# Attention in two-chunk operations over adjacent PSUM banks, with PSUM as one tile and operands in 4 KB pairs

## The chip, the cores and the metric

One core of one Trainium2 chip runs the whole program. The metric is the device time of an execution in microseconds; the time given for a kernel is the median of its runs. TensorE appears in the profile as PE (matmuls) and PEld (weight loads), VectorE as DVE, ScalarE as ACT, GpSimd as POOL, and SyncE, which issues the DMAs, as SP.

## What is computed

Two batches of 3008 tokens go through an attention without softmax and then through two feed-forward layers (256 to 2048 to 256), all in float32.

```python
def _attn_ref(u, v, z):
    scores = (1.0 / S) * np.matmul(z, z.transpose(0, 2, 1))   # S = 3008, z has 64 columns
    attn = np.maximum(scores, 0.0) ** 2
    return u * np.matmul(attn, v)                             # v and u have 256 columns

def _moe_ref(x, w_in, w_out):
    h = x @ w_in
    return np.where(h > 0.0, h, np.exp(np.minimum(h, 0.0)) - 1.0) @ w_out

def _moe2_ref(x, w_in, w_out, a, b):
    h = x @ w_in
    P = a[0] + a[1] * h + a[2] * h**2 + a[3] * h**3
    Q = 1.0 + np.abs(b[0]) * np.abs(h) + np.abs(b[1]) * h**2
    return (P / (Q + 1e-06)) @ w_out
```

## The kernel before

Each float32 operand of a matmul is held as a rounded part (hi, r) and a remainder (lo, l), and each product is three matmuls (hi times hi, lo times hi, hi times lo). So most of the work of the other engines is making such pairs.

*Attention.* The queries are cut into 12 tiles (`spans`), six per batch, of 512 columns; the sixth of each batch has 448. The keys are cut into 24 chunks of 128 rows, the last half full; a step n is one chunk of one tile, and there are NA = 288 steps. The 64 channels of z lie twice on the partitions, so scores for two chunks run on the two row halves of PE at once. At every even step `pair` (L249) issues the six score matmuls for chunks n and n+1 into two banks of PSUM. `scores` (L263) then does for one chunk: ScalarE's relu (L270, PSUM to SBUF), ScalarE's square of it (L273, the hi part), and VectorE's product of score and relu (L277), written over the score in PSUM, for the first eight chunks into SBUF. One step later `scores_lo` (L281) subtracts the hi part from that product (L285, VectorE), which gives the lo part and leaves the bank free. `values` (L288) follows LAG = 4 steps behind the scores: twelve matmuls per chunk (L303), six in the half-full one, into four banks, one for each half of the model columns and each row half. At the end of a tile VectorE multiplies two of these banks by u (L309), ScalarE copies the two others (L310), POOL multiplies and adds (L312, L313) and the tile is stored to DRAM (L314).

*Weights.* Each weight arrives as 64-bit words and is turned into a pair by ScalarE (L177, L194, L195), VectorE (the words step L181 and L183, the powers step L188 and L190, one chunk step apart) and POOL (L199 to L206). 32 half-megabyte pieces are spread over the attention steps by a list of due steps, `todo`: 12 of them during the first batch, between the second batch's values, stored to DRAM and read back by `stages_reload` from step NA on, and 20 directly during the second batch, straight into the pool `wp` of 64 operands of 2 KB per partition. That pool also holds the values, as hi and lo.

*Feed-forward.* 13 token tiles (384, ten of 512, two of 256 columns) go through both layers in one pipeline of steps (`ffn_step`, L563); a step has one group of 128 hidden rows of the first layer and, three steps behind the tile, one of the second. Line numbers: `hidden` L358 (L363, L364, L366), `project` L369 (through L231 to L233), the first layer's exponential L390 and L391, ELU L396 and split L402 (ScalarE) and L403 (POOL), the second's polynomial L436 to L493. The last tile's steps are put in order by a small planner (`finish`).

*Order.* The program is written under a manual schedule: each engine executes its instructions in the order in which the code issues them. In step n that is scores(n), scores_lo(n-1), what `todo` holds for n, values(n-4), then the feed-forward step. PSUM's eight banks come from a pool of eight one-bank tiles; SBUF operands come from small pools by tag (x 6, rl 4, x2 4, hi 3, lo 3, r 2, q 3, e 3, t 3 of 2 KB).

```python
    for n in range(NA + NSTEP):
        if n < NA:
            scores(n)
        if 0 < n <= NA:
            scores_lo(n - 1)
        for fn in todo.pop(n, ()):
            fn()
        if LAG <= n < NA + LAG:
            values(n - LAG)
```

## Time and profile before

| | |
|---|---|
| median of 3 runs | 1635.21 us (1633.59 to 1637.61) |
| the profiled execution | 1636.99 us |
| its span in the profile | 1635.2 us |
| mean granted clock of PE | 0.988 |
| PE busy | 1582.3 us (97%), 9240 matmuls |
| DVE busy | 1407.3 us (86%), 2148 instructions |
| ACT busy | 1342.6 us (82%), 2321 |
| POOL busy | 751.5 us (46%), 595 |
| DMA | 63.46 MB in 40000 packets, 12.1% of 16 engines |

Busy time is the union of an engine's instructions. Matmuls are pipelined and their ends are modelled, so a PE that is shown busy may still be waiting in part; two matmuls on the two row halves run at once and are shown as two overlapping instructions. A wait is put down to the instruction that ended last before it. Clock 1.00 is the full granted clock.

### The profile page before, as it was taken

To read this page: it belongs to the slowest core of one execution; us is meant where nothing else is said; L and a number is where in the kernel's file an instruction comes from. 1 tells how busy PE (TensorE), PEld (TensorE's weight loads), DVE (VectorE), ACT (ScalarE), POOL (GpSimd) and SP (SyncE) were. 2 spreads that over 40 slices of the span, in tenths; PEclk is the share of its full clock that TensorE was granted. 3 is DMA by queue.
4 is the path that set the end of the run, shared out by engine and by line. 5 is a ranking of instruction groups with operands and counts; after the bars stand their busy time and mean duration, and the time that the engine had idled before them with its cause. 6 is when DMAs were issued, how large, how long until landed. Compare 5 with 4: busy or idle time off the path is not lost.

```text
span 1635.2 us, 25774 instructions
## 1 busy us (share of the span) xinstructions
PE 1582.3 (97%) x9240; PEld 1299.7 (79%) x9240; DVE 1407.3 (86%) x2148; ACT 1342.6 (82%) x2321; POOL 751.5 (46%) x595
## 2 busy tenths in 40 slices
PE   8999999999999999999999999999999999998897
PEld 6877778777878878878878787878788787887796
DVE  7788888998987368888898989898898989899998
ACT  7788777787886688989888888888898888887796
POOL 3334341433443445444444544444444445447645
PEclk9999999999999999999999999999999999999998
DMA  4223233112221410000000000000000000000000
GB/s 129 71 93 127 87 112 118 58 54 72 78 78 48 140 52 1 23 1 27 1 1 27 1 26 1 27 0 27 0 27 1 1 20 1 20 0 14 1 14 13
DMA packets 40128, 65.09 MB, mean 40 GB/s; under 512 B 5440, under 2 KB 18240, under 8 KB 40000
## 3 DMA queue, kind: packets, MB, share of 16 engines
q1 hardware_dynamic: 40000, 63.46, 12.1%
q8 instruction: 72, 1.18, 0.3%
q14 instruction: 56, 0.46, 0.1%
HBM read 44.83 MB, written 18.61 MB: 39 GB/s over the span
## 4 chain that ended last, share of the span: by engine, by line
PE 69%; DVE 11%; ACT 4%; issue 3%; POOL 1%; DMA 0%; POOLq 0%; DVEq 0%; ACTq 0%
PE acc L232 10%; PE acc L233 10%; PE h L363 10%; PE h L364 10%; PE acc L231 10%; PE h L366 10%; PE acc L303 9%; PE s L259 3%; DVE lo L285 1%; DVE s L277 1%; DVE x L486 1%; ACT e L270 1%; DVE q L465 1%; DVE raw L181 1%; DVE t L488 1%
## 5 line engine op out<-in xcount | busy, mean ns | idle before, releaser
L493 POOL TENSOR_TENSOR x<-t,r 128x512 fp32r<-128x512 f32 (+1 forms) x190 | 250.2, 1317 | 479.3 <-DVE t L488 459.3
L303 PE MATMUL acc<-hi,v 64*128 64x512 f32 (+1 forms) x1364 | 255.0, 393 | 3.9 <-DVE x L285 2.3
L403 POOL TENSOR_TENSOR lo<-e,hi 128x512 fp32r<-128x512 f32 (+1 forms) x192 | 246.0, 1282 | 24.9 <-ACT hi L402 24.9
L277 DVE SCALAR_TENSOR_TENSOR s<-s,e 128x512 f32<-128x512 f32 (+1 forms) x280 | 191.4, 684 | 64.6 <-ACT e L270 60.9
L270 ACT ACTIVATE e<-s 128x512 f32<-128x512 f32 (+1 forms) x288 | 167.0, 580 | 74.1 <-PE s L259 72.2
L436 ACT ACTIVATE t<-h,coef 128x512 f32<-128x512 f32 (+1 forms) x192 | 148.0, 771 | 82.5 <-PE h L366 82.4
L303 PEld LDWEIGHTS acc<-hi,v 64*128 64x128 f32 x1364 | 188.8, 187 | 31.8 <-DVE xo L309 3.2
L303 PE MATMUL acc<-lo,v 64*128 64x512 f32 (+1 forms) x682 | 204.8, 391 | 1.2 <-DVE lo L285 1.2
L463 DVE SCALAR_TENSOR_TENSOR q<-q,coef,h 128x512 f32<-128x512 f32 (+1 forms) x166 | 122.0, 735 | 83.3 <-ACT q L456 83.3
L303 PE MATMUL acc<-r,v 64*128 64x512 f32 (+1 forms) x892 | 166.8, 390 | 5.0 <-DVE lo L285 3.3
L232 PE MATMUL acc<-x,w 128*128 128x512 f32 (+2 forms) x416 | 158.2, 380 | 7.7 <-POOL x L493 7.5
L232 PE MATMUL acc<-lo,w 128*128 128x512 f32 (+2 forms) x416 | 157.7, 379 | 5.2 <-POOL lo L403 4.9
L363 PE MATMUL h<-x,w 128*128 128x512 f32 (+2 forms) x416 | 155.2, 376 | 5.0 <-DVE t L488 5.0
L231 PE MATMUL acc<-x,w 128*128 128x512 f32 (+2 forms) x416 | 157.1, 378 | 3.1 <-DVE t L488 3.1
L233 PE MATMUL acc<-x,w 128*128 128x512 f32 (+2 forms) x416 | 157.2, 378 | 0.0
L363 PE MATMUL h<-rl,w 128*128 128x512 f32 (+2 forms) x416 | 154.9, 376 | 2.3 <-DVE e L396 1.6
L233 PE MATMUL acc<-hi,w 128*128 128x512 f32 (+2 forms) x416 | 156.2, 375 | 0.0
L231 PE MATMUL acc<-hi,w 128*128 128x512 f32 (+2 forms) x416 | 156.0, 375 | 0.0
L364 PE MATMUL h<-x,w 128*128 128x512 f32 (+2 forms) x416 | 155.2, 376 | 0.0
L364 PE MATMUL h<-rl,w 128*128 128x512 f32 (+2 forms) x416 | 154.5, 375 | 0.0
L396 DVE SCALAR_TENSOR_TENSOR e<-e,h 128x512 f32<-128x512 f32 (+1 forms) x192 | 128.5, 669 | 27.1 <-ACT e L391 27.1
L303 PEld LDWEIGHTS acc<-r,v 64*128 64x128 f32 x892 | 122.6, 184 | 23.7 <-ACT q L310 3.5
(107 smaller groups left out, 4416.2 us busy)
## 6 DMA issues: line engine op xcount, KB each, us to landing
raw<-w_in_dram SPq DMA_DIRECT2D x16, 512.0 KB, 4.0
raw<-w_out_dram SPq DMA_DIRECT2D x16, 512.0 KB, 4.6
wd<-q SPq DMA_DIRECT2D x24, 256.0 KB, 2.3
raw<-wd SPq DMA_DIRECT2D x12, 512.0 KB, 3.4
raw<-v_dram SPq DMA_DIRECT2D x22, 256.0 KB, 3.7
raw<-uT_dram SPq DMA_DIRECT2D x10, 512.0 KB, 4.2
xd<-xo SPq DMA_DIRECT2D x20, 256.0 KB, 2.0
outT_dram<-xo SPq DMA_DIRECT2D x20, 256.0 KB, 2.1
```

The costliest lines, as they stand in the source:

```text
L231: nc.tensor.matmul(out, lhsT=lh, rhs=rh, start=start, stop=False)
L232: nc.tensor.matmul(out, lhsT=lh, rhs=rl, start=False, stop=False)
L233: nc.tensor.matmul(out, lhsT=ll, rhs=rh, start=False, stop=stop)
L270: nc.scalar.activation(p[:, :w], s[:, :w], AF.Relu, scale=SCALE)
L277: nc.vector.scalar_tensor_tensor(out=q[:, :w], in0=s[:, :w], scalar=SCALE, in1=p[:, :w], op0=ALU.mult, op1=ALU.mult)
L303: nc.tensor.matmul(acc[ti][d][h][:, :w], lhsT=lhs[rows, j % 2, d * P:(d + 1) * P], rhs=rhs[rows, :w], start=j == 0 and k == 0, stop=j >= N ...
L363: nc.tensor.matmul(h[:, cols], lhsT=wh[:, d, c], rhs=x[d][0], start=d == 0, stop=False)
L364: nc.tensor.matmul(h[:, cols], lhsT=wl[:, d, c], rhs=x[d][0], start=False, stop=False)
L366: nc.tensor.matmul(h[:, cols], lhsT=wh[:, d, c], rhs=x[d][1], start=False, stop=d == ND - 1)
L403: nc.gpsimd.tensor_tensor(out=lo, in0=e, in1=f(hi), op=ALU.subtract)
L436: act(new("p", "t", 3), h, AF.Identity, bias=a2, scale=a3)
L493: tt(out=st["lo"], in0=st["p"], in1=st["r"], op=ALU.mult)
```

## The change

The two chunks of a pair get one operation each for relu, square, product and subtraction, 1024 columns over two adjacent banks (512 per bank). PSUM becomes one tile of eight banks. During attention scores use banks 0 to 3 in turn (n % 4) and the accumulators 4 to 7; in the feed-forward part the kernel hands banks out from a list and takes them back after the last reader (`bank`, `give`), and where the list is empty before `first_hidden`, the ELU is issued ahead of it. All operand buffers become pairs of 4 KB: `wp` has 32 of them, and the relu's output is taken from there. The tile's accumulators are read in two halves: two banks before the matmuls of its last chunk, two after. The last tile's four final operations run on VectorE in place of POOL. 18 weight pieces are kept directly and 14 stored and read back, from step NA-4 on; the first feed-forward input is split at step NA-3 in place of NA-1.

```diff
-    wp = ctx.enter_context(tc.tile_pool(name="wp", bufs=64))
+    wp = ctx.enter_context(tc.tile_pool(name="wp", bufs=32))
...
-    ps = ctx.enter_context(tc.tile_pool(name="ps", bufs=8, space=bass.MemoryType.PSUM))
+    ps = ctx.enter_context(tc.tile_pool(name="ps", bufs=1, space=bass.MemoryType.PSUM))
...
+    def sb2(tag, bufs, dt=F32R):
+        return sp.tile([P, 2, W], dt, tag=tag, bufs=bufs, name=tag)
+
+    def wide(dt=F32R):
+        return wp.tile([P, 2, W], dt, tag="w", name="w")
+
+
+    psum = ps.tile([P, 8, W], F32, tag="psum", name="psum")
+    free_banks = []
+    banks_of = {}
+
+    def bank(key):
+        i = free_banks.pop(0)
+        banks_of.setdefault(key, []).append(i)
+        return psum[:, i]
+
+    def give(key):
+        free_banks.extend(banks_of.pop(key))
...
-            r = sb("x", 6, F32R)
-            l = sb("rl", 4, F32R) if s < 4 else sb("t", 3, F32R)
+            if s < 4:
+                rl = sb2("rl", 2) if s < 2 else sb2("x2", 2)
+                r, l = rl[:, 0], rl[:, 1]
+            else:
+                r, l = (sb("t", 3, F32R) if s == 4 else sb("r", 2, F32R) for _ in range(2))
...
+            if keep:
+                st["t"] = wide()
+            st["hi"] = st["t"][:, 0] if keep else sb("q", 3, F32R)
...
-    def pair(n):
+    def scores(n):
 
         ti, j = divmod(n, NCH)
         bb, i0, w = spans[ti]
         r, l = Z[bb, i0 // W]
         sr, sl = Z[bb, j // 4]
-        out = sc[n], sc[n + 1] = bank("s"), bank("s")
+        i = n % 4
+        s = psum[:, i:i + 2, :w]
         for k, (lhs, rhs) in enumerate(((sr, r), (sl, r), (sr, l))):
             for h in range(2):
                 rows, c = slice(h * DQ, (h + 1) * DQ), (j + h) % 4 * P
-                nc.tensor.matmul(out[h][:, :w], lhsT=lhs[rows, c:c + P], rhs=rhs[rows, :w], start=k == 0, stop=k == 2)
-
-    sc = {}
-
-    def scores(n):
-        ti, j = divmod(n, NCH)
-        bb, i0, w = spans[ti]
-        if j % 2 == 0:
-            pair(n)
-        s = sc.pop(n)
-        p = sb("e", 3)
-        nc.scalar.activation(p[:, :w], s[:, :w], AF.Relu, scale=SCALE)
-        spare = n % (LAG + 1) > 2
-        hi = sb("r", 2, F32R) if spare else sb("hi", 3, F32R)
-        nc.scalar.activation(hi[:, :w], p[:, :w], AF.Square)
-
-
-        q = sb("t", 3) if n < 8 else s
-        nc.vector.scalar_tensor_tensor(
-            out=q[:, :w], in0=s[:, :w], scalar=SCALE, in1=p[:, :w], op0=ALU.mult, op1=ALU.mult)
-        hl[n] = hi, q
+                nc.tensor.matmul(s[:, h], lhsT=lhs[rows, c:c + P], rhs=rhs[rows, :w], start=k == 0, stop=k == 2)
+        hi = sb2("hl", 3)
+        e = wide(F32)[:, :, :w]
+        nc.scalar.activation(e, s, AF.Relu, scale=SCALE)
+        nc.scalar.activation(hi[:, :, :w], e, AF.Square)
+
+        nc.vector.scalar_tensor_tensor(out=s, in0=s, scalar=SCALE, in1=e, op0=ALU.mult, op1=ALU.mult)
+        hl[n] = hi
 
     def scores_lo(n):
         w = spans[n // NCH][2]
-        hi, q = hl[n]
-        lo = sb("x2", 4, F32R) if n % (LAG + 1) > 2 else sb("lo", 3, F32R)
-        nc.vector.tensor_tensor(out=lo[:, :w], in0=q[:, :w], in1=f(hi[:, :w]), op=ALU.subtract)
-        hl[n] = hi, lo
+        hi, lo = hl.pop(n), sb2("x", 3)
+        i = n % 4
+        nc.vector.tensor_tensor(
+            out=lo[:, :, :w], in0=psum[:, i:i + 2, :w], in1=f(hi[:, :, :w]), op=ALU.subtract)
+        for h in range(2):
+            hl[n + h] = hi[:, h], lo[:, h]
+        if n >= NA - 4:
+            free_banks.extend((i, i + 1))
 
     def values(n):
         ti, j = divmod(n, NCH)
         bb, i0, w = spans[ti]
         if j == 0:
 
-            acc[ti] = [[bank("acc") for _ in range(2)] for _ in range(ND)]
+            acc[ti] = {way: psum[:, 4 + k] for k, way in enumerate(((1, 0), (0, 1), (0, 0), (1, 1)))}
         hi, lo = hl.pop(n)
         vh, vl = V[bb, j // 2]
-
-
-        ways = ((0, 1), (1, 0)) if j < NCH - 1 else ((0, 1),)
-        for way in ways:
+        if j == NCH - 1:
+            xd[ti] = dp.tile([P, ND, W], F32, tag=f"xd{ti}", name=f"xd{ti}")
+            out_of(ti, 1, w)
+
+
+        for way in ((1, 0), (0, 1))[j == NCH - 1:]:
             for k, (lhs, rhs) in enumerate(((vh, hi), (vl, hi), (vh, lo))):
                 for h, d in enumerate(way):
                     rows = slice(h * P // 2, (h + 1) * P // 2)
-                    nc.tensor.matmul(acc[ti][d][h][:, :w], lhsT=lhs[rows, j % 2, d * P:(d + 1) * P], rhs=rhs[rows, :w],
-                                     start=j == 0 and k == 0, stop=j >= NCH - 2 and k == 2 and (h != d or j == NCH - 1))
+                    nc.tensor.matmul(
+                        acc[ti][d, h][:, :w], lhsT=lhs[rows, j % 2, d * P:(d + 1) * P], rhs=rhs[rows, :w],
+                        start=j == 0 and k == 0, stop=k == 2 and j == NCH - 1 - (h != d))
         if j == NCH - 1:
-            xd[ti] = dp.tile([P, ND, W], F32, tag=f"xd{ti}", name=f"xd{ti}")
-            x, y = [sb("xo", 2)[:, :w] for _ in range(ND)], [sb("q", 3)[:, :w] for _ in range(ND)]
+            x, y = out_of(ti, 0, w)
+
+            eng = nc.gpsimd if ti < NTL - 1 else nc.vector
             for d in range(ND):
-                nc.vector.tensor_tensor(out=x[d], in0=acc[ti][d][0][:, :w], in1=us[ti][:, d, :w], op=ALU.mult)
-                nc.scalar.copy(y[1 - d], acc[ti][1 - d][1][:, :w])
-            for d in range(ND):
-                nc.gpsimd.tensor_tensor(out=y[d], in0=y[d], in1=us[ti][:, d, :w], op=ALU.mult)
-                nc.gpsimd.tensor_tensor(out=x[d], in0=x[d], in1=y[d], op=ALU.add)
+                eng.tensor_tensor(out=y[d], in0=y[d], in1=us[ti][:, d, :w], op=ALU.mult)
+                eng.tensor_tensor(out=x[d], in0=x[d], in1=y[d], op=ALU.add)
                 nc.sync.dma_start(out=xd[ti][:, d, :w], in_=x[d])
-            del acc[ti], us[ti]
+            del acc[ti], us[ti], sums[ti]
...
+    sums = {}
+
+    def out_of(ti, d, w):
+
+        x, y = sums.setdefault(ti, ({}, {}))
+        x[d], y[1 - d] = sb("xo", 2)[:, :w], (sb("t", 3) if d else sb("e", 3))[:, :w]
+        nc.vector.tensor_tensor(out=x[d], in0=acc[ti][d, 0][:, :w], in1=us[ti][:, d, :w], op=ALU.mult)
+        nc.scalar.copy(y[1 - d], acc[ti][1 - d, 1][:, :w])
+        if ti == NTL - 1:
+            free_banks.extend((4, 5) if d else (6, 7))
+        return x, y
...
-        hi, lo = ([sb("rl", 4, F32R)[:, :w] for _ in range(ND)] for _ in range(2))
+        hi, lo = ([t[:, d, :w] for d in range(ND)] for t in (sb2("rl", 2), sb2("rl", 2)))
...
-        hi, lo = sb("hi", 3, F32R)[:, :flat(i)], sb("lo", 3, F32R)[:, :flat(i)]
+        t = sb2("hl", 3)
+        hi, lo = t[:, 0, :flat(i)], t[:, 1, :flat(i)]
...
-            new("hi", "x", 6, F32R)
+            two(("hi", "lo"), wide() if last else sb2("x", 3))
...
+        reads = {"linear", "size", "denominator", "numerator"} if plain else {"quotient"}
+
+        def then_free(name, fn):
+            def run():
+                fn()
+                if name in reads:
+                    reads.remove(name)
+                    if not reads:
+                        give(("h", 1, i))
+            return run
...
+        elu = [i1] if i1 else []
         if i:
+            if not free_banks:
+                first_elu(elu.pop())
...
-    direct, stored = order[:NF + 4], order[NF + 4:]
-    halves = [x for pair in zip(((1, g) for g in range(NCH // 2)), stored) for x in pair]
+    direct, stored = order[:NF + 2], order[NF + 2:]
+    halves = [x for g, key in enumerate(stored) for x in ([(1, g), key] if g < NCH // 2 else [key])]
...
-        at(NA + 3 * k // 2, AHEAD, stages_reload(*key))
+        at(NA - 4 + 3 * k // 2, AHEAD, stages_reload(*key))
...
-        if n < NA:
+        if n < NA and n % 2 == 0:
             scores(n)
-        if 0 < n <= NA:
+        if n < NA and n % 2:
...
-        if n == NA - 1:
+        if n == NA - 3:
```

## Rows read from the trace of the kernel before

**Rows 1.** Stretches: length, busy us per engine (count), granted clock, DMA share, GB/s
```profile
5.13:538.30 533.17, 512.70 (x4267) 416.50 (x4268) 456.32 (x754) 413.13 (x727) 207.57 (x167) 0.99 0.27 86
538.30:620.00 81.70, 76.57 (x372) 69.11 (x373) 46.76 (x83) 64.08 (x126) 40.84 (x37) 0.96 0.26 90
620.00:1300.00 680.00, 679.70 (x2935) 547.89 (x2934) 604.76 (x896) 593.40 (x1008) 323.35 (x253) 1.00 0.04 11
...
1590.00:1636.00 46.00, 34.28 (x236) 32.35 (x236) 37.92 (x55) 28.50 (x49) 24.45 (x19) 0.87 0.04 12
```

**Rows 2.** Chain that ended last, 300 to 340 us: start, us, what
```profile
304.62 0.69 PE s L259 x6
305.31 2.79 PE acc L303 x24
```

**Rows 3.** Who waited for whom, 20 to 560 us: total, times, longest
```profile
PEld s L259 <- DVE lo L285: 14.8, 21, 2.1
...
PEld s L259 <- DVE x L285: 8.1, 14, 1.0
...
PEld acc L303 <- DVE xo L309: 6.2, 10, 2.0
```

**Rows 4.** Stretches: the start; three of the eleven tile turns, and their sum
```profile
5.13:30.15 25.02, 22.55 (x163) 15.95 (x163) 22.44 (x35) 20.10 (x36) 10.22 (x8) 1.00 0.49 141
...
96.26:100.80 4.54, 4.22 (x34) 2.89 (x32) 4.38 (x9) 4.34 (x8) 2.86 (x3) 1.00 0.07 23
...
182.74:190.61 7.87, 5.55 (x32) 3.89 (x30) 6.43 (x12) 4.56 (x9) 4.42 (x4) 0.78 0.09 34
...
494.09:500.58 6.49, 5.44 (x33) 4.01 (x30) 5.25 (x10) 5.05 (x10) 6.33 (x6) 0.76 0.01 3
sum 59.61, PE 49.33 PEld 34.33 DVE 55.48 ACT 48.39 POOL 42.84; mean PE 4.48 PEld 3.12 DVE 5.04 ACT 4.40 POOL 3.89
```

**Rows 5.** Timeline of one pair: start, us, engine, line, [idle before <- releaser]
```profile
177.16 0.39 PE L303 MATMUL acc<-hi,v 64*128 64x512 f32 x1
...
177.36 0.60 ACT L270 ACTIVATE e<-s 128x512 f32<-128x512 f32 x1 [1.00 <-PE s L259]
...
177.99 0.70 DVE L277 SCALAR_TENSOR_TENSOR s<-s,e 128x512 f32<-128x512 f32 x1 [0.93 <-ACT e L270]
...
178.60 0.68 DVE L285 TENSOR_TENSOR lo<-s,hi 128x512 fp32r<-128x512 f32 x1
...
179.20 0.69 DVE L277 SCALAR_TENSOR_TENSOR s<-s,e 128x512 f32<-128x512 f32 x1
```

**Rows 6.** Groups by line and shape: busy us, mean ns, idle before, releasers
```profile
L277 DVE SCALAR_TENSOR_TENSOR s<-s,e 128x512 f32<-128x512 f32 x232 | 161.3, 695 | 51.8 <-ACT e L270 48.1
...
L270 ACT ACTIVATE e<-s 128x512 f32<-128x512 f32 x240 | 141.3, 589 | 60.4 <-PE s L259 59.3
...
L285 DVE TENSOR_TENSOR lo<-s,hi 128x512 fp32r<-128x512 f32 x138 | 93.9, 681 | 0.0
...
L277 DVE SCALAR_TENSOR_TENSOR s<-s,e 128x448 f32<-128x448 f32 x48 | 30.1, 628 | 12.9 <-ACT e L270 12.8
...
L270 ACT ACTIVATE e<-s 128x448 f32<-128x448 f32 x48 | 25.7, 536 | 13.7 <-PE s L259 12.9 <-DVE rl L119 0.8
...
L181 DVE SCALAR_TENSOR_TENSOR raw<-q,raw 128x512 f32<-128x512 f32 x32 | 24.3, 759 | 0.0
...
L183 DVE TENSOR_SCALAR q<-raw 128x512 uint32<-128x512 uint32 x32 | 18.5, 578 | 2.3
```

**Rows 7.** Timeline at the end of attention, POOL and PE
```profile
543.06 1.19 POOL L313 TENSOR_TENSOR xo<-xo,q 128x448 f32<-128x448 f32 x1
...
544.22 1.94 POOL L403 TENSOR_TENSOR lo<-e,hi 128x384 fp32r<-128x384 f32 x2
...
545.26 0.69 PE L232 MATMUL acc<-lo,w 128*128 128x384 f32 x1 [2.50 <-POOL lo L403]
```

**Rows 8.** Timeline in the late feed-forward part, one matmul
```profile
1477.50 0.39 PE L363 MATMUL h<-rl,w 128*128 128x256 f32 x1 [1.62 <-DVE e L396]
```

More of the change, by code (lines that the diff above doesn't have):

```diff
@@ L147, in split @@
             raw = st["raw"]
-            hi, lo = (wp.tile([P, 2, DM], F32R, tag="w", name="v") for _ in range(2))
+            t = wide()
+            hi, lo = (t[:, i].rearrange("p (c d) -> p c d", c=2) for i in range(2))
             nc.scalar.copy(hi, raw)
@@ L221, in copy @@
         def copy():
-            hl = [wp.tile([P, W], F32R, tag="w", name="w") for _ in range(2)]
+            t = wide()
+            hl = [t[:, i] for i in range(2)]
             nc.scalar.copy(hl[0], st["raw"][:, 0])
@@ L357, in hidden @@
     def hidden(which, x, i):
-        h = bank("h")
+        h = bank(("h", which, i))
         for k, cols in blocks(i):
@@ L372, in project @@
         if n == 0:
-            acc[which, ti] = [bank("acc") for _ in range(ND)]
+            acc[which, ti] = [bank(("acc", which, ti)) for _ in range(ND)]
         steps = [(d, k, cols) for k, cols in blocks(i) for d in range(ND)]
@@ L410, in split_x2 @@
             p = acc[0, ti][d][:, :w]
-            hi, lo = (sb("x2", 4, F32R)[:, :w] for _ in range(2))
+            t = sb2("x2", 2)
+            hi, lo = t[:, 0, :w], t[:, 1, :w]
             nc.scalar.copy(hi, p)
@@ L414, in split_x2 @@
             x2[ti].append((hi, lo))
+        give(("acc", 0, ti))
     def second_hidden(i):
@@ L433, in new, with two @@
             return st[key]
+        def two(keys, t):
+            for i, key in enumerate(keys):
+                st[key] = t[:, i, :n]
         def linear():
@@ L439, in square @@
             if last:
-                new("s", "s2", 0), new("r", "r", 0)
+                two("sr", wide(F32))
             elif late(i):
@@ L450, in size @@
             if last:
-                st["q"] = bank("q")[:, :n]
+                st["q"] = bank(("h", 1, i))[:, :n]
             else:
@@ L505, in second @@
             ]
-        return [
+            return listed()
+        steps = [
             ("square", "A", 0.85, ["hidden"], square),
@@ L516, in second @@
         ]
+        return listed()
     def late(i):
```

21 lines of the change are left out of this document (10 added, 11 removed).

## The prediction

> **What bounds the kernel now.** I read the stretches first, then the chain of waits, then who waited for whom, then single instructions. The stretches [rows 1] cut the span at the first scores matmul, at the end of the last attention matmul and at the stalls of the end. In the middle of the feed-forward part PE is busy 679.70 of 680 us: nothing that this change does on other engines can shorten that. In the attention stage PE shows 512.70 of 533.17 us, but the ends of matmuls are modelled, so I price the stage from the chain: where it runs freely, two chunks cost 0.69 us of scores and 2.79 us of values [rows 2], 3.48 us. A tile is 12 such pairs less three matmul pairs (the half chunk at its end, 0.70), 41.1 us; the two tiles of 448 columns come to about 36.2 (448/512 of it and a little). Ten and two make 483.4 us; the stretch also holds about 3 us of early feed-forward matmuls. So attention loses 533.2 - 483.4 - 3.2 = **46.6 us** to waits of PE, and that is all the change can win there.
>
> Where are they? PE waits before scores for VectorE's L285, 14.8 and 8.1 us in 35 times, and before values for L309, 6.2 us [rows 3]. Eleven tile turns, each from the fifth chunk's scores to the seventh's, take 59.61 us together, the wide ones between 4.54 and 7.87 each [rows 4]; nine cost 3.48 and two narrow ones about 3.06 without waits, 37.4 in all, so the turns lose **22.2 us**. The other 24.4 us are the start (25.02 us [rows 4] for two scores and five pairs, 18.8: some 6) and single waits in the middle of tiles (some **18**).
>
> Why single waits? Follow one pair [rows 5]. PE goes on from scores to values at 177.16, the relu starts at 177.36, the product at 177.99, the subtraction that stands next on VectorE at 178.60, 0.61 later, and it lasts about 0.68. That subtraction empties the second of the two banks that the next scores want (L285 of the chunk before), so the next scores can start 0.20 + 0.63 + 0.61 + 0.68 = 2.12 us after PE left the last ones, and PE wants them after 2.79. **The slack is 0.6 us.** A weight's word step on VectorE (L181 and L183, 0.759 + 0.578 [rows 6]) is more than that, so nearly each one becomes a PE wait.
>
> **The change, part by part.** *Wide operations.* From 448 to 512 columns the product grows by 67 ns and the relu by 53 [rows 6]. Carried on to 1024: relu 0.589 + 8 x 0.053 = 1.01, product 0.695 + 8 x 0.067 = 1.23, subtraction by the same slope 0.681 + 0.54 = 1.22 us. No row has a two-bank operation: at best it costs this, at worst twice the single (1.18, 1.39, 1.36). I take the slope, since nothing in a row depends on the bank, and keep the other end for the range. Per pair of chunks VectorE's four operations start 0.60 to 0.61 apart [rows 5], 2.41 us; the two wide ones take 1.23 + 1.22 less the same 0.08 each of overlap, 2.29. That frees only 0.12 x 144 = 17 us of VectorE, and it is no term of the sum, as PE is the bound.
>
> The Trainium skill, "VectorE: DVE Perf Modes", section "The DRAIN you can't avoid", says that a VectorE operation does not start until the pipeline of the one before is empty, and advises few operations. By that rule each operation removed would give back its whole fixed part, 2 x 0.15 us a pair, 44 us in all; the starts 0.61 apart of operations that last 0.68 to 0.70 speak against it.
>
> *Order and banks.* Scores now use four fixed banks in turn, and both subtractions of a pair are one operation, a step later than its scores. Scores n need banks that were emptied by the subtraction of pair n-4. From the moment PE leaves scores n-4: relu at 0.20, product at 1.24, subtraction from 2.39 to 3.61; PE comes back to these banks after 2 x 3.48 - 0.69 = 6.27. **The slack grows from 0.6 to 2.6 us**, more than one weight step in two adjacent chunk steps (1.34 and about as much) leaves over once VectorE's free 1.2 us of a pair is taken off. If two weights lay closer, or a step were held up by POOL, some wait would stay. Of the 18 us I take 14 away; bounds 18 and 4. The intermediate is released in pairs too (three each), which the two-pair lag covers, and the relu's output goes to the weights' pool, where two slots are left at the fullest point: the product of the pair before the last has then long ended.
>
> *Start.* First relu 0.42 later, product no longer in an extra buffer, both fractions of a microsecond: 6 us become 5.5, bounds -2 and +2.
>
> *Tile turn.* The accumulators now keep four fixed banks. Before the last half chunk the kernel issues the two reads that empty banks 4 and 5, and the new tile starts on these. On VectorE that read stands behind the subtraction: from PE leaving scores, subtraction done at 3.61, read from 3.53 to 4.21; PE has 1.40 of values, 0.70 of the half chunk and 0.69 of scores in between and wants bank 4 at 2.79. So each turn waits about 1.45 us. The shortest turn now waits 4.54 - 3.48 = 1.06 [rows 4]: **the turn itself gets longer, not shorter**. On top come weight steps that the new spacing (18 kept, 14 stored) puts between product and read: by the step numbers in the code, words at turn 2, the second batch's first queries at turn 6, words and powers at turns 8 and 10. The now longest turn (182.74, words and powers in the same place) lost 4.39 us at a granted clock of 0.78 [rows 4], so I take 4.7 each for turns 8 and 10, 2.65 for 2 and 6, 1.45 for seven others: 24.9 against 22.2, **+2.7**; bounds -6 and +10.
>
> *Last tile on VectorE.* POOL's four operations of the last tile end at 544.22 and hold up L403; PE waits 2.50 us for it and its next matmuls are slower [rows 7]. Four operations of about 0.62 on VectorE (L285's 0.681 [rows 6] less the 0.067 of the slope) put 2.5 us in front of the third group's L396 instead, so that its L403 ends near 544 rather than 545.2. With the clock kept, 2 to 3.5 us are won; bounds -1 (they delay L396 and nothing is won) and +4. I take **-2.5**.
>
> The Trainium skill, "SBUF — State Buffer", section "Who interferes with whom", says that a VectorE instruction with two SBUF inputs and a GpSimd instruction that reads SBUF exclude each other for a whole instruction. By that these four could be held by one or two L403, a microsecond each, and the sum would be -12.5 in place of -15.
>
> *The rest.* Where no bank is free the ELU goes ahead of the hidden matmuls that need its bank: one such wait of 1.62 us stands in the late part [rows 8], and VectorE had one other operation in front: -0.7, bounds 0 and -2. Two more reloads (a DMA, a ScalarE and a VectorE copy each) fall in the first 20 feed-forward steps, four steps earlier than now, with VectorE 46.76 busy of 81.70 there [rows 1]: nothing. Splitting the first feed-forward input two steps earlier costs three VectorE operations in front of a subtraction with 2.6 us of slack: nothing. The pairs in the feed-forward part and the 4 KB slots at the tail hold as many operands as before but free them together; bounds -1 and +3 on the last 46 us [rows 1].
>
> Sum: -14 - 0.5 + 2.7 - 2.5 - 0.7 = **-15.0 us**. The profiled execution took 1636.99 us for its span of 1635.2, 1.8 above the median of the three runs, 1635.21. So 1622.0 on its own terms, and **1620** for a median.
>
> **The rivals.** *VectorE was the stage's bound.* Then fewer operations give it back by the rule above, all single waits, the weight steps in the turns and the start's idle time go: -18 - 4 - (22.2 - 11 x 1.45 = 6.2) - 4 - 1 = -33, 1602. For it: 456.32 of 533.17 us busy, and more in the second half. Against: PE runs whole stretches at 3.48 with VectorE waiting for the relu. *The single waits stay*, because wide operations cost twice the single ones and hold the queue in larger lumps: subtraction done at 0.20 + 1.18 + 1.39 + 1.36 = 4.1, slack 2.1, turn 2.0; the gain of 14 falls to about 6, the turns cost +8, and with -3.2 for the rest the time is within 2 us of now, about 1634. The same would be seen if the compiled kernel still held two operations. *Slower: the tile turn.* One mechanism: fixed accumulator banks make each new tile wait behind the subtraction, and the clock falls after it. The two turns at 0.78 and, in the last tile, 0.76 lost 4.4 and 3.4 us, those that waited about 1 us kept the clock [rows 4]. It decides once the turns lose 22.2 + 17.7 = 40 us, 3.6 each; at 4.4 each they lose 48, +26 - 17.7, and the time is 1645. For it: nothing doubles the accumulators. Against: by the steps only two turns get there. *One tile guarded as a whole:* if each matmul waited for any read of the one PSUM tile, scores could start only after the pair before is subtracted, 3.6 us instead of 2.79 after PE left it, 144 x 0.8 = +117 in attention alone, 1750. Against: the kernel tells banks apart by slices; no row can show it.
>
> **How the numbers follow.** The forecast has a chance of 0.62, VectorE as the bound 0.13, waits that stay 0.14, the turn 0.08, the whole guard 0.03. The forecast's own bounds run from about -26 to -4. A difference of 0.3% (5 us) is what a measurement here can tell from no change. Of the forecast nearly all is faster by more; with the first rival faster has 0.75, within 0.3% 0.14, slower 0.11. For 8 in 10 the range reaches to the first rival's 1602 and on the other side to 1632, into the waits that stay.
>
> **What the profile would show.** Right: relu, product and subtraction at two banks of about 1.01, 1.23 and 1.22 us, 144 times each; waits of scores for L285's successor nearly gone; pairs of 3.48 us inside tiles; each turn some 1.5 us longer than that; no POOL operation of the last tile; attention ended near 525 us; the feed-forward stretches as they are. Wrong: two-bank durations near twice the single; turns of 7 us and a clock under 0.9 in them; a new wait inside the feed-forward middle, where now there is none.

## The result and the profile after

The changed kernel takes **1644.57 us** (median of 4 runs, 1643.74 to 1645.75) against 1635.32 us (4 runs, 1633.59 to 1637.61) for the kernel before in the same comparison: a ratio of **1.0056 [1.0039, 1.0074]**, 9.25 us slower. The profiled execution took 1645.2 us, its span is 1643.4 us. Line numbers of the changed kernel: scores L283, relu L286, square L287, product L289, subtraction L296, values L320, the tile's reads L339 (VectorE) and L340 (ScalarE), its final operations L328 and L329, the words step L201 and L203, the powers step L208 and L210, the ELU L424, its split L433, the second layer's matmuls L254 to L256.

The same stretches as in [rows 1], cut at the first scores matmul and, within 0.1 us, at the end of the last attention matmul:

```profile
4.79:549.17 544.38, 509.27 (x4266) 447.99 (x4266) 445.42 (x470) 374.54 (x441) 206.91 (x167) 0.97 0.28 88
549.17:620.00 70.83, 67.23 (x341) 59.80 (x340) 41.67 (x75) 57.62 (x114) 32.24 (x29) 1.00 0.33 104
620.00:1300.00 680.00, 679.43 (x2938) 548.01 (x2938) 604.00 (x897) 593.50 (x1010) 323.25 (x253) 1.00 0.04 11
```

Attention takes 544.38 us where it took 533.17 [rows 1]: **+11.2**. From its end to the end of the span it is 1643.4 - 549.17 = 1094.2 us against 1635.2 - 538.30 = 1096.9: **-2.7**. The middle is as it was. So the whole loss lies in attention, with 284 VectorE instructions fewer (754 to 470).

The eleven tile turns, each cut as in [rows 4], from the fifth chunk's scores to the seventh's:

```profile
53.51:58.86 5.35, 3.72 (x33) 2.99 (x30) 5.14 (x6) 3.17 (x5) 3.55 (x3) 1.00 0.03 11
96.44:106.06 9.62, 6.12 (x32) 4.91 (x30) 9.17 (x10) 4.94 (x8) 5.86 (x5) 0.65 0.08 30
143.71:152.55 8.84, 6.18 (x33) 4.35 (x29) 6.26 (x8) 3.83 (x6) 4.68 (x4) 0.69 0.40 120
...
276.25:284.90 8.65, 5.06 (x32) 4.01 (x30) 7.16 (x8) 3.30 (x5) 4.54 (x4) 0.80 0.09 29
...
365.43:375.93 10.50, 6.01 (x32) 4.85 (x30) 8.11 (x10) 4.38 (x7) 5.81 (x5) 0.67 0.07 25
413.53:421.00 7.47, 5.28 (x33) 4.54 (x30) 7.23 (x8) 4.32 (x6) 6.88 (x6) 0.77 0.09 35
458.58:468.35 9.77, 5.28 (x32) 4.43 (x30) 8.11 (x10) 4.38 (x7) 5.09 (x4) 0.83 0.07 27
505.80:512.60 6.80, 4.87 (x33) 4.52 (x30) 5.17 (x6) 3.94 (x6) 6.56 (x6) 0.75 0.12 41
sum 82.58, PE 53.54 PEld 43.90 DVE 71.29 ACT 42.76 POOL 55.69; mean PE 4.87 PEld 3.99 DVE 6.48 ACT 3.89 POOL 5.06
```

They take 82.58 us where they took 59.61, so they lose 82.58 - 37.4 = 45.2 in place of 22.2: **+23.0**. Only the four turns that nothing disturbs (the first and three not shown) keep the full clock. What is left of attention, the tiles' insides and the start, is 11.2 - 23.0 = **-11.8**: there the change does most of what it was forecast to do. The start has no part in it: to the eighth pair's scores it takes 25.05 us (4.79 to 29.84) where it took 25.02. The chain of waits runs at 3.48 a pair as in [rows 2], and of the waits for the subtraction, 14.8 and 8.1 us in [rows 3], little is left; the turn's reads (L339) have become the first cause of PE's waits. Who waited for whom, 20 to 560 us:

```profile
PE psum L320 <- DVE xo L339: 28.0, 11, 4.5
...
PEld psum L283 <- DVE x L296: 4.8, 5, 2.0
...
PE psum L283 <- DVE x L296: 3.1, 3, 1.6
```

A turn that meets nothing else, the first one, by the timeline:

```profile
52.68 1.23 DVE L289 SCALAR_TENSOR_TENSOR psum<-psum,w 128x1024 f32<-128x1024 f32 x1 [0.92 <-ACT w L286]
...
53.51 0.84 PE L283 MATMUL psum<-rl 64*128 64x512 f32 x6
...
54.01 1.23 DVE L296 TENSOR_TENSOR x<-psum,hl 128x1024 fp32r<-128x1024 f32 x1
...
55.16 1.28 DVE L339 TENSOR_TENSOR xo<-psum,raw 128x512 f32<-128x512 f32 x2
...
55.98 0.72 PE L320 MATMUL psum<-hl,w 64*128 64x512 f32 x4 [1.63 <-DVE xo L339]
```

Product, subtraction and reads stand in one row on VectorE, and PE, done with the scores at 54.35, waits for the first read until 55.98. Turn 2 has the same row with a weight's words step in it:

```profile
96.96 1.23 DVE L296 TENSOR_TENSOR x<-psum,hl 128x1024 fp32r<-128x1024 f32 x1
...
98.10 1.49 DVE L201 SCALAR_TENSOR_TENSOR raw<-q,raw 128x512 f32<-128x512 f32 x1
...
99.63 0.43 DVE L203 TENSOR_SCALAR q<-raw 128x512 uint32<-128x512 uint32 x1
99.97 1.28 DVE L339 TENSOR_TENSOR xo<-psum,raw 128x512 f32<-128x512 f32 x2
...
100.80 1.22 PE L320 MATMUL psum<-hl,w 64*128 64x512 f32 x4 [3.50 <-DVE xo L339]
```

The words step puts the reads 1.87 us later, PE waits 3.50 us, and the pair of values that follows runs at half speed, as one more stretch shows:

```profile
100.80:106.06 5.26, 5.26 (x24) 4.46 (x26) 4.95 (x5) 1.21 (x2) 4.60 (x4) 0.50 0.15 55
```

At a granted clock of 0.50, the lower of the two levels (1.2 GHz), 24 matmuls take 5.26 us instead of 2.79 [rows 2]: here the wait costs another 2.5 us after it has ended.

### The profile page after: what moved, and what is told of

It reads as the page before. It is cut to its first block, busy times and chain, and to the rows that moved or that the text cites. A ratio compares the mean times of both kernels' runs of the same rounds, so it can differ in the third digit from the quotient of the medians.

```text
span 1643.4 us, 25037 instructions
## 1 busy us (share of the span) xinstructions
PE 1574.1 (96%) x9240; PEld 1324.9 (81%) x9240; DVE 1396.5 (85%) x1866; ACT 1303.5 (79%) x2035; POOL 746.3 (45%) x591
## 4 chain that ended last, share of the span: by engine, by line
PE 63%; DVE 12%; ACT 5%; issue 3%; POOL 1%; POOLq 0%; DVEq 0%; ACTq 0%
PE psum L320 11%; PE psum L255 8%; PE psum L391 8%; PE psum L392 8%; PE psum L394 8%; PE psum L256 8%; PE psum L254 8%; PE psum L283 3%; DVE x L521 2%; DVE t L523 1%; DVE e L424 1%; DVE q L500 1%; DVE q L522 1%; DVE psum L289 1%; POOL hl L433 1%
## 5 line engine op out<-in xcount | busy, mean ns | idle before, releaser
L320 PE MATMUL psum<-hl,w 64*128 64x512 f32 (+1 forms) x2256 | 377.8, 398 | 29.0 <-DVE xo L339 28.0
L320 PEld LDWEIGHTS psum<-hl,w 64*128 64x128 f32 x2256 | 246.7, 190 | 62.2 <-ACT w L286 12.6
L433 POOL TENSOR_TENSOR hl<-e,hl 128x512 fp32r<-128x512 f32 (+1 forms) x192 | 246.2, 1282 | 31.3 <-ACT hl L432 30.2
L320 PE MATMUL psum<-x,w 64*128 64x512 f32 (+1 forms) x1128 | 247.4, 395 | 0.0
L286 ACT ACTIVATE w<-psum 128x1024 f32<-128x1024 f32 (+1 forms) x144 | 145.0, 1007 | 127.8 <-PE psum L283 126.4
L289 DVE SCALAR_TENSOR_TENSOR psum<-psum,w 128x1024 f32<-128x1024 f32 (+1 forms) x144 | 173.9, 1207 | 78.0 <-ACT w L286 77.7
L296 DVE TENSOR_TENSOR x<-psum,hl 128x1024 fp32r<-128x1024 f32 (+1 forms) x144 | 172.9, 1201 | 11.6 <-ACT q L197 0.5
L255 PE MATMUL psum<-hl,w 128*128 128x512 f32 (+2 forms) x416 | 157.4, 378 | 3.1 <-POOL hl L433 2.7
L391 PE MATMUL psum<-x,w 128*128 128x512 f32 (+2 forms) x416 | 154.2, 374 | 5.5 <-DVE t L523 5.5
L391 PE MATMUL psum<-rl,w 128*128 128x512 f32 (+2 forms) x416 | 154.3, 374 | 2.3 <-DVE e L424 1.6
L254 PE MATMUL psum<-hl,w 128*128 128x512 f32 (+2 forms) x416 | 155.8, 374 | 0.5 <-ACT hl L432 0.5
L256 PE MATMUL psum<-hl,w 128*128 128x512 f32 (+2 forms) x416 | 155.6, 374 | 0.0
L287 ACT ACTIVATE hl<-w 128x1024 fp32r<-128x1024 f32 (+1 forms) x144 | 150.5, 1045 | 4.6
L392 PE MATMUL psum<-rl,w 128*128 128x512 f32 (+2 forms) x416 | 153.9, 373 | 0.0
L392 PE MATMUL psum<-x,w 128*128 128x512 f32 (+2 forms) x416 | 153.8, 373 | 0.0
L255 PE MATMUL psum<-x,w 128*128 128x512 f32 (+2 forms) x384 | 147.2, 383 | 3.8 <-POOL x L527 3.7
L254 PE MATMUL psum<-x,w 128*128 128x512 f32 (+2 forms) x384 | 146.7, 382 | 3.1 <-DVE t L523 3.1
L424 DVE SCALAR_TENSOR_TENSOR e<-e,psum 128x512 f32<-128x512 f32 (+1 forms) x192 | 128.5, 669 | 22.3 <-ACT e L419 22.3
L256 PE MATMUL psum<-x,w 128*128 128x512 f32 (+2 forms) x384 | 146.6, 382 | 0.0
```

Of the source, the lines that this page charges most:

```text
L254: nc.tensor.matmul(out, lhsT=lh, rhs=rh, start=start, stop=False)
L255: nc.tensor.matmul(out, lhsT=lh, rhs=rl, start=False, stop=False)
L256: nc.tensor.matmul(out, lhsT=ll, rhs=rh, start=False, stop=stop)
L287: nc.scalar.activation(hi[:, :, :w], e, AF.Square)
L289: nc.vector.scalar_tensor_tensor(out=s, in0=s, scalar=SCALE, in1=e, op0=ALU.mult, op1=ALU.mult)
L296: nc.vector.tensor_tensor(out=lo[:, :, :w], in0=psum[:, i:i + 2, :w], in1=f(hi[:, :, :w]), op=ALU.subtract)
```

## The experiments

Ratios are to the kernel before on the same chip, with their 95% intervals; "turns" is the sum of the eleven turns in the profiled execution (before 59.61, after 82.58). The first four start from the changed kernel, the fifth from the one before. The runs come from three chips, on which the kernel before took 1633.91 to 1635.41 us (1635.32 in the comparison above), so differences between medians are given by the ratios too where that matters.

**The turn's values, with their reads, ahead of the subtraction.**

```diff
+        turn = LAG <= n < NA and (n - LAG) % NCH == NCH - 1
+        if turn:
+            values(n - LAG)
         if n < NA and n % 2:
             scores_lo(n - 1)
...
-        if LAG <= n < NA + LAG:
+        if LAG <= n < NA + LAG and not turn:
             values(n - LAG)
```

> The changed kernel, with one thing moved: at each tile turn the matmuls of the last half chunk and the four reads that empty the accumulator banks are issued ahead of the wide subtraction and of the weight steps of that chunk step. Theory (the changed kernel is slower because its accumulators have no other banks to go to, so each turn waits for reads that stand behind the subtraction and the weight steps on VectorE, and a wait of over 2 us then costs clock too): the eleven turns, 82.6 us in the changed kernel, fall to about 48 to 55 (0.5 us of wait each, about 2 where a weight step stands ahead of the subtraction), the granted clock is 1.00 in nearly all of them, and the time is 1610 to 1616. Rival (the wide operations themselves or the two-bank scores make the turn long, whatever stands ahead): the turns stay over 70 us and the time over 1630.

1619.17 us, 0.9909 [0.9894, 0.9924]; turns 53.17. The forecast of the turns came, the time a little above its range: the turns fell by 29.4 us, but the single waits for the subtraction rose, from 4.8 us in 5 times to 9.8 in 11. Who waited for whom in this kernel, 20 to 560 us:

```profile
PE psum L320 <- DVE xo L339: 10.1, 10, 2.5
PEld psum L283 <- DVE x L296: 9.8, 11, 2.4
```

Turn 2 of this kernel, by the timeline, which is to be read against the one above:

```profile
96.44 1.28 DVE L339 TENSOR_TENSOR xo<-psum,raw 128x512 f32<-128x512 f32 x2
...
97.27 0.91 PE L320 MATMUL psum<-hl,w 64*128 64x512 f32 x4 [0.28 <-DVE xo L339]
...
97.64 1.21 DVE L296 TENSOR_TENSOR x<-psum,hl 128x1024 fp32r<-128x1024 f32 x1
...
98.77 0.68 DVE L201 SCALAR_TENSOR_TENSOR raw<-q,raw 128x512 f32<-128x512 f32 x1
```

The same operations in another order: PE waits 0.28 us in place of 3.50. The reads' place behind the subtraction (and the words step) cost 1644.57 - 1619.17 = 25.4 us, 24.0 by the ratios.

**Weight steps kept out of the turns** (every direct or stored piece due in the middle of a tile, steps 5 to 21 as the diff counts them).

```diff
             n = n0 + k * (n1 - n0) // len(each)
+            j = (n + 5) % NCH
+            if len(key) == 3 and not 5 <= j <= 21:
+                n += 5 - j if j < 5 else 21 - j
```

> The changed kernel, with the due steps of the weights shifted by up to seven chunk steps so that no word or power step falls on the chunks 22, 23 and 0 to 4 of a tile; the reads stay where they are. Theory: every turn costs what the undisturbed ones cost (5.35 us, 1.87 over a free pair), 11 of them about 58 us in place of 82.6; the turns with the second batch's query splits stay long; the time is 1618 to 1626. Rival (weight steps have no part in it, the waits come from the order of reads alone): turns near 80, time near 1643.

1625.2 us, 0.9948 [0.9932, 0.9965]; turns 62.26, and all but the second batch's first (9.71) at a clock of 1.00, as the theory had it. Meetings of turns and weights cost 19.4 us, 17.7 by the ratios.

**Each two-bank operation as two of one bank**, in the changed kernel's order.

```diff
-        nc.scalar.activation(e, s, AF.Relu, scale=SCALE)
+        for h in range(2):
+            nc.scalar.activation(e[:, h], s[:, h], AF.Relu, scale=SCALE)
...
-        nc.vector.tensor_tensor(
-            out=lo[:, :, :w], in0=psum[:, i:i + 2, :w], in1=f(hi[:, :, :w]), op=ALU.subtract)
+        for h in range(2):
+            nc.vector.tensor_tensor(
+                out=lo[:, h, :w], in0=psum[:, i + h, :w], in1=f(hi[:, h, :w]), op=ALU.subtract)
```

(square and product in the same way)

> The changed kernel, with each operation over two banks split into two of 512 columns (relu, relu, square, square, product, product, subtraction, subtraction); banks, order of the pairs, pools and reads stay. Theory (what removed the single waits inside tiles is the later subtraction and the longer way back to the same banks, not the width): pairs inside tiles stay at 3.48 us, turns stay near 80 us, the time is within 5 us of the changed kernel's 1644. Rival (fewer and wider operations on VectorE are what removed the single waits): waits of scores for the subtraction come back, some 12 to 18 us, and the time is 1656 or more.

1630.41 us, 0.9979 [0.9969, 0.9988]; turns 67.80. Neither my theory (width hardly matters) nor the rival came: **the width itself costs 13 to 14 us** (12.6 by the ratios, 14.2 by the medians), all of it in the turns (82.58 - 67.80 = 14.8). The single waits stay away without it:

```profile
PEld psum L283 <- DVE x L301: 4.9, 8, 1.6
```

**The last tile's final operations back on POOL.**

```diff
-            eng = nc.gpsimd if ti < NTL - 1 else nc.vector
+            eng = nc.gpsimd
```

> The changed kernel, with the four final operations of the last attention tile back on POOL. Theory (they held up POOL's split of the first feed-forward groups): PE waits for that split again after the last values, 2 to 3 us and some clock, and the time is 1 to 4 us above the changed kernel's, 1646 to 1648. Rival (the place makes no difference, since VectorE holds the ELU back as long): within 1 us of it.

1645.0 us, 1.0065 [1.005, 1.008]: the total decides nothing, since attention itself ended 5.7 us earlier in the profiled execution (turns 2, 3 and 6 were 0.9, 2.6 and 1.3 us shorter there; in turn 3 PE's second wait was 0.61 us in place of 1.04 and the clock stayed at 1.00). So the same attention gives

```profile
sum 77.71, PE 49.10 PEld 40.64 DVE 68.49 ACT 42.80 POOL 51.49; mean PE 4.46 PEld 3.69 DVE 6.23 ACT 3.89 POOL 4.68
```

of turns in one execution and 82.58 in another: sums of turns, each from one execution, that lie less than 5 us apart are not told from each other by that alone, and by this execution the turns grew by 18.1 us and not by 23.0. The stage decides, at the end of attention, by the timeline of this kernel:

```profile
543.52 0.45 PE L254 MATMUL psum<-hl,w 128*128 128x384 f32 x1
...
550.67 0.44 PE L255 MATMUL psum<-hl,w 128*128 128x384 f32 x1 [2.54 <-POOL hl L433]
```

From the first of these to the end of its span, 1640.2, it is 1096.7 us; in the changed kernel, from the same matmul at 549.17, 1094.2. The wait of 2.50 us of [rows 7] is back as 2.54.

**The kernel before with fixed halves of PSUM**: four banks for scores and hidden, four for accumulators, in attention and afterwards (the last tile's planner without the store's two banks).

```diff
-        return ps.tile([P, W], F32, tag="bank", name=name)
+        tag = "acc" if name == "acc" else "bank"
+        return ps.tile([P, W], F32, tag=tag, bufs=4, name=name)
...
```

> The kernel BEFORE the change with one part of it alone: its eight PSUM banks are split into four for scores (and hidden rows) and four for accumulators, so that a new tile's accumulators can only take the banks of the old one, as in the changed kernel. Operations, their order, the reads at the turn and all SBUF pools stay as before (the planner of the tail may use four banks where it had six). Theory (fixed accumulator banks are what makes the turns long): the single waits inside tiles stay as they were, the eleven turns go from 59.6 us to 68 to 80, and the time rises by 8 to 20 us, to 1642 to 1654. Rival (a new tile had no other banks before either, since the four others held scores; the turns are long only by the wide operations and where the weights fall): turns 58 to 63, time within 4 us of the kernel before.

1644.13 us, 1.0053 [1.0038, 1.0069]; turns 65.19. The time looks like the theory's, but two stretches of this kernel, attention and the tail, say otherwise:

```profile
5.13:538.30 533.17, 512.23 (x4266) 427.46 (x4266) 455.92 (x755) 413.09 (x727) 207.94 (x167) 0.99 0.27 86
...
1590.00:1643.00 53.00, 35.08 (x230) 32.85 (x228) 37.33 (x52) 27.17 (x47) 24.39 (x19) 0.85 0.03 11
```

The last attention matmuls start at 537.93, before's at 537.85: the turns lose 5.6 us more (2.7 of them in turn 7 alone, 6.60 to 9.27) and the rest of attention wins as much. The 8 us are in the tail (35.08 us of PE in 53, against 34.28 in 46 [rows 1]), where the split of the banks binds the planner; the changed kernel has no such split there. So fixed accumulator banks lengthen a free turn a little (4.54 to 4.83), go with 5.6 of the 23.0 us by which the turns grew, and are not the main part of what made them long. My theory fell here.

**Single operations in the order of before**: one chunk per step, its subtraction a step later; PSUM and 4 KB pairs as in the changed kernel.

```diff
...
         if n < NA and n % 2 == 0:
             scores(n)
-        if n < NA and n % 2:
+        if n < NA:
+            chunk(n)
+        if 0 < n <= NA:
             scores_lo(n - 1)
```

> The changed kernel with its operations split into single chunks and also in the order of the kernel before: relu, square and product of one chunk per chunk step, its subtraction one step later, so that the second bank of a pair is emptied a step later than in the changed kernel. Banks, pairs, reads and weights stay as in the changed kernel. Theory (the early subtraction of both chunks gave the slack that removed the single waits): waits of scores for the subtraction come back, 12 to 18 us of them, in the middle of tiles, and the time is 1640 to 1650, 10 or more above the singles of the last round (1630). Rival (the fixed score banks alone gave it, in whatever order): the middle of the tiles stays free, time 1626 to 1634.

1640.34 us, 1.0031 [1.002, 1.0042]; turns 68.05, the same as with single operations in pairs (67.80), and yet 9.9 us longer (8.5 by the ratios). The single waits are back. Who waited for whom, 20 to 560 us:

```profile
PEld psum L283 <- DVE x L306: 17.4, 29, 2.1
```

Against 4.8 us in 5 times after, and 4.9 in 8 with single operations in the changed order. What removed them was the order (both chunks' operations at the even step, both subtractions at the next), **not the width**.

**Reads first and weights away**, both diffs above.

> The changed kernel with both repairs: the turn's reads ahead of the subtraction, and no weight step near a turn. Theory (the two add up, where each left what the other takes): ten turns at 4.0 us, the one with the query split near 7.5, 48 us together, granted clock 1.00 but in that one; time 1608 to 1613, 6 to 11 below the reads alone. Rival (weights shifted off the turns press on each other and wait elsewhere): single waits of 5 us or more in the middle of tiles and 1616 or more.

1609.27 us, 0.9845 [0.9828, 0.9863]; turns 46.43, both as the theory had them.

**Reads first, weights away and single operations**, all three.

> The same two repairs, and every two-bank operation split into two of 512 columns. Theory (width costs only the longer way through relu, product and subtraction, which the turn no longer waits for once the reads stand ahead of the subtraction): turns 3.6 to 4.0, time within 4 us of the wide version with both repairs. Rival A (width still costs where the product stands ahead of the reads, about 0.5 us a turn): 5 to 6 us faster than it. Rival B (the extra operations on VectorE and ScalarE press inside tiles): slower by 4 us or more.

**1603.58 us, 0.9805 [0.9791, 0.982]**; turns 40.17 of at least 37.4. The rival with a cost of width came, 5.7 us faster than the wide one. This is the fastest kernel here, 1.95% ahead of before. Its first turn and the one turn that still loses more:

```profile
53.92:57.55 3.63, 3.63 (x34) 3.46 (x31) 3.63 (x8) 3.21 (x7) 2.78 (x3) 1.00 0.00 0
...
260.61:265.48 4.87, 3.92 (x34) 3.27 (x32) 4.84 (x10) 3.34 (x7) 3.64 (x3) 1.00 0.07 25
```

**The kernel before with weights away** (the due-step diff alone).

> The kernel BEFORE the change, with the due steps of its weights shifted as in the second run, so that no word or power step falls on the chunks 22, 23 and 0 to 4 of a tile. Theory now (the weights' places matter at any turn, but the wide operations make each meeting dearer: the changed kernel won 19 us by this shift): the eleven turns go from 59.6 us to 50 to 53, where the undisturbed ones lie (4.54, the narrow one 3.9, the one with the query split 5.6); single waits inside tiles stay or grow a little; the time falls by 4 to 9 us, to 1626 to 1631. Rival (the kernel before loses as much by its weights' places as the changed one, and the shift would win 15 us or more): 1620 or less.

1629.22 us, 0.997 [0.9959, 0.9981]; turns 49.67. This is the theory's time. Here the meetings cost 9.9 us of turns and 4.7 of time; the weight steps moved into the tiles make longer single waits there (the scores' weight loads wait 24.8 us for L285 in 35 times, before 22.9 in 35).

**Single operations and weights away**; then **single operations and reads first.**

> The changed kernel with its two-bank operations split into singles and the weights shifted off the turns; the reads stay behind the subtraction. Theory (width adds 0.5 us to each undisturbed turn and about as much again or more where a weight step falls on it): turns of 4.8 us, one near 6, 53 us together, time 1614 to 1619, 6 to 10 us below the wide version with the same shift (1625). Rival (width costs only where weights fall on a turn): within 4 us of that version.

1615.84 us, 0.989 [0.9873, 0.9906]; turns 53.01.

> The changed kernel with singles and with the reads ahead of the subtraction; the weights stay. Theory: undisturbed turns of 3.6 us, those with weight steps between product and read 5 to 6; time 1608 to 1614, 5 to 11 below the wide version with the same reads (1619). Rival (with the reads ahead, width costs nothing): within 3 us of it.

1609.29 us, 0.9846 [0.9832, 0.9861]; turns 42.97. Both as forecast. Together:

| | turns, weights as placed | turns, weights away | difference |
|---|---|---|---|
| before | 59.61 | 49.67 | 9.9 |
| after, wide | 82.58 | 62.26 | 20.3 |
| after, single | 67.80 | 53.01 | 14.8 |
| reads first, wide | 53.17 | 46.43 | 6.7 |
| reads first, single | 42.97 | 40.17 | 2.8 |

Width lengthens the turns in every pair of rows, and most where the reads stand behind the subtraction and a weight step meets them. Followed from kernel to kernel, the turns go from 59.61 before to 65.19 with fixed halves, 68.05 with single operations in the order of before on the changed kernel's banks, pairs and weights, 67.80 with the changed order and 82.58 with the width. So 14.8 of the 23.0 us go with the width (9.9 of 18.1 by the other execution of the wide attention) and 5.6 with the fixed banks; the other 2.6 (weights in new places, pairs of 4 KB) were not separated, and the last two are within the spread of one attention.

## Why the prediction was wrong

The forecast of 1620 failed on one term, **the tile turn: +2.7 forecast, +23.0 measured**. That the turn gets longer, because its read stands behind the subtraction, was seen; its size was not. The rival "Slower: the tile turn" is what came: turns that lose 48 (45.2 measured), 1645 (1644.57). It got 0.08. That its time is right to the microsecond is luck, since its turns lost 2.8 us too much and the gains set against them (17.7, with 14.5 measured) were 3.2 us too large; and of its mechanism, fixed banks and then the clock, the banks go with 5.6 of the 23.0 us. Against 24.9 forecast, the 45.2 are: four undisturbed turns 7.4 in place of 5.8, the four turns named as disturbed 24.6 in place of 14.7, three more 13.1 in place of 4.35. What the term had wrong:

- *The free turn.* A wait of 1.45 was forecast, a turn of 4.93; it takes 5.35, 1.87 over 3.48. The subtraction was made to start 0.08 before the product's end, as neighbours do in [rows 5]. There the neighbours belong to different chunks; here the subtraction needs the product just before it and starts 1.33 us after it, 0.10 behind its end. The read, which needs neither, starts 1.15 after the subtraction. PE starts 0.82 after the first read does, 0.14 more than the 0.68 forecast.
- *Which turns are disturbed.* Four were named (2, 6, 8, 10). All four were, but so were 3, 9 and 11. In turn 3 ScalarE waited 2.56 us for a weight's DMA ahead of the turn's copies, so that PE waited a second time, 1.04 us, for L340. In 9 and 11 a powers step one step earlier put the subtraction back (ScalarE's part of it, L216 and L217, held up the relu, so that the product started 0.6 us later), PE waited 2.19 and 1.93 us in place of 1.63, and the clock of the turn fell to 0.77 and 0.75.
- *The price of a meeting.* 4.7 for turns 8 and 10 and 2.65 for 2 and 6 were taken from a row of before; measured over 3.48 they lost 7.0 and 6.3, 6.1 and 5.2. In that row, 182.74 in [rows 4], PE waited 1.34 and 0.97 us in two pieces, with a few matmuls between; here it waits 3.50 in turn 2 and 4.49 in turns 8 and 10 in one, since the wide subtraction and the weight steps stand together in front of the read, and the loss of clock, which that row had too, comes on top. Against the rival stood that "only two turns get there", to 3.6 us; seven did (2, 3, 6 and 8 to 11), and the average came to 4.1.

The other terms. **Single waits: -14 forecast, with the start -14.5; measured -11.8**, with nothing at the start. The reason given was right, by the run in the order of before. Of its 2.6 us of slack about 2.4 were there (scores at 50.73, their subtraction done at 55.24, the banks wanted again two pairs, 6.96 us, after 50.73), and they came from the order, which single operations have as well. **Wide operations:** 1.01, 1.23 and 1.22 us forecast, measured by groups and shape

```profile
L289 DVE SCALAR_TENSOR_TENSOR psum<-psum,w 128x1024 f32<-128x1024 f32 x120 | 147.6, 1230 | 67.5 <-ACT w L286 67.2
L296 DVE TENSOR_TENSOR x<-psum,hl 128x1024 fp32r<-128x1024 f32 x120 | 146.7, 1223 | 9.9 <-ACT q L197 0.5
...
L286 ACT ACTIVATE w<-psum 128x1024 f32<-128x1024 f32 x120 | 123.0, 1025 | 110.4 <-PE psum L283 110.2
```

The sizes were right and the reading of them was not. As a term they were put at nothing because VectorE isn't the bound; the free turn carried their lengths ("subtraction from 2.39 to 3.61"), but no price was put on what they add where a weight step meets the row from scores to read. The first product can't start until both banks have been through the relu (1.03 in place of 0.59), and the subtraction no longer overlaps. Nor does VectorE win in a pair: 1.33 + 1.15 = 2.48 from the product's start to the start of what follows the subtraction, where four single operations take 2.41 from start to start. **Last tile: -2.5 forecast**, 2.5 by the stage. **ELU: -0.7 forecast, nothing measured**: PE still waits 1.64 us for L424, as in [rows 8] for L396. The change did not move the ELU there: its input, the exponential L419, was done at 1480.32, and VectorE came to it without a pause, behind the same two operations of the second layer's polynomial as before (L500 and L508, before L465 and L473).

```profile
1479.69 0.63 ACT L419 ACTIVATE e<-e 128x512 f32<-128x512 f32 x1
...
1483.05 0.75 DVE L508 SCALAR_TENSOR_TENSOR psum<-psum,coef,t 128x512 f32<-128x512 f32 x1
...
1483.71 0.67 DVE L424 SCALAR_TENSOR_TENSOR e<-e,psum 128x512 f32<-128x512 f32 x1
...
1484.44 0.39 PE L391 MATMUL psum<-rl,w 128*128 128x256 f32 x1 [1.64 <-DVE e L424]
```

Last tile and ELU together were to give -3.2, and the part behind attention gave -2.7. The rest cost nothing, as forecast; no wait appeared in the feed-forward middle.

Of the two rules weighed. The Trainium skill, "VectorE: DVE Perf Modes", section "The DRAIN you can't avoid", taken as the prediction took it, would have given 44 us of VectorE for the operations removed. The section itself adds that a next operation that is not held starts earlier, and the advice of few operations stands in the page's "Rules for kernel authors". VectorE's busy time in attention fell by 456.32 - 445.42 = 10.9 us, and independent neighbours overlap by 0.08, so the rows agree with the addition and not with the bare rule. For an operation that uses the one before, the bare rule describes what the first turn shows, a start 0.10 behind the end. The Trainium skill, "SBUF — State Buffer", section "Who interferes with whom", has a VectorE operation with two SBUF inputs and a GpSimd operation that reads SBUF exclude each other. In the last tile nothing of that cost time (the four finals took 0.62 to 0.63 us), but in turn 2 of the changed kernel L201, which has two such inputs, took 1.49 us (mean 0.723), and POOL's L328 was running for its first 0.95. There the trace agrees, and it was 0.8 us of the 3.50 that I hadn't priced.

What stays open: how much of a long turn is the wait and how much the clock was separated only in turn 2 (about 3.5 and 2.5 us) and turn 6 (below); why the same wait took the clock in one execution and not in another; why attention of the kernel with POOL's final operations varied between executions; and whether another plan for the tail would spare the fixed halves their 8 us.

## What to carry to other kernels

A wider operation that saves no time on the bounding engine can still make a chain that runs through it longer, so price it at the place where the chain is in the open (a buffer's turnover), and not in the steady part. Where one engine's queue holds both work with slack and the one read that frees a buffer for the bounding engine, issue the read first: here a change of order with no operation less was worth 24 to 25 us, some nine times what the turn was forecast to cost. And price a wait that meets another by counting the operations in the row before the release, with the pair at the lower clock as the upper end.

## What the runs showed of the hardware

What a wait costs in clock does not follow from its length alone. In the first turn 1.63 us left it at 1.00, in turns 11 and 9 1.93 and 2.19 us went with 0.75 and 0.77 over the turn, in turn 3 1.62 and 1.04 with 0.69, and 3.50 us in turn 2 was followed by a stretch at 0.50. So turn 2 waited twice as long as turn 1 and lost 6.1 against 1.9 us. But turns 8 and 10, which both waited 4.49 us, show 0.67 and 0.83, and turn 6, with one and the same row of operations, waited 3.59 to 3.60 us in three kernels: the changed one (8.65 us at 0.80, above), the one with POOL's final operations, and the one with the weights away. PE's first matmul after the wait, in this order, and turn 6 of the last two:

```profile
280.70 1.22 PE L320 MATMUL psum<-hl,w 64*128 64x512 f32 x4 [3.59 <-DVE xo L339]
...
276.35 0.74 PE L320 MATMUL psum<-hl,w 64*128 64x512 f32 x4 [3.60 <-DVE xo L339]
...
271.36 1.22 PE L320 MATMUL psum<-hl,w 64*128 64x512 f32 x4 [3.60 <-DVE xo L339]
...
271.90:279.23 7.33, 3.73 (x33) 3.13 (x30) 7.17 (x8) 3.31 (x5) 3.41 (x4) 1.00 0.06 19
...
266.90:276.61 9.71, 6.12 (x33) 4.87 (x30) 7.17 (x8) 3.31 (x5) 4.51 (x4) 0.65 0.11 39
```

The same wait cost 1.3, 0 and 2.4 us of clock, in the order of the kernels above, and the 2 us from which the first experiment's theory let a wait cost clock are no limit that these rows bear out (1.93 us lost it, 3.60 kept it). The gain of moving a read can be larger than the wait that it removes, then, but not by a fixed factor: with reads first the waits for L339 fell by 28.0 - 10.1 = 17.9 us and the turns by 29.4.

With reads first and weights away the wide kernel's turn 6 still loses 3.9 us (7.35 less 3.48). Its timeline shows the exclusion of VectorE and GpSimd in front of the read that matters:

```profile
265.20 1.13 POOL L328 TENSOR_TENSOR t<-t,raw 128x448 f32<-128x448 f32 x1 [11.95 <-DVE t L137]
265.24 1.63 DVE L138 TENSOR_TENSOR t<-e,t 128x512 fp32r<-128x512 f32 x1
266.80 1.14 DVE L339 TENSOR_TENSOR xo<-psum,raw 128x448 f32<-128x448 f32 x2
267.55 0.74 PE L320 MATMUL psum<-hl,w 64*128 64x512 f32 x4 [2.45 <-DVE xo L339]
```

L138 splits the second batch's query tile and took 0.69 us in the fastest kernel's turn 6, where POOL's multiplication started 0.34 us after it; here POOL starts 0.04 us ahead of it, and it takes 1.63, straight in front of the reads. PE waited 2.45 us here and 0.94 there. An operation with one SBUF input was stretched as well: in turns 8 and 10 of the changed kernel L203 took 1.37 us beside POOL's L328, in place of 0.43 in turn 2, and this stood in front of the read too.
